# A written-out program order for every engine in the attention part of a fused attention and mixture-of-experts kernel

## The chip, the cores and the metric

The kernel runs on one core of a Trainium2 chip. The metric is the device time of one execution in microseconds (us), the median over several executions.

The engines are named as in the profile: PE is TensorE (PEld its weight loads), DVE is VectorE, ACT is ScalarE, POOL is GpSimd, and SP is the queue that issues most DMA transfers. Each engine takes its instructions in one order; engines wait for each other through semaphores.

## The reference

A decaying linear attention over 4 batches, 8 heads, 768 positions and head size 48, in float32, feeds a mixture of 8 experts of which each token takes one.

```python
def _attn_ref(q, k, v, alpha):
    for t in range(S):
        state = alpha[:, :, t, :, None] * state + np.einsum('bhd,bhe->bhde', k[:, :, t], v[:, :, t])
        y[:, :, t] = np.einsum('bhd,bhde->bhe', q[:, :, t], state)
...
def _moe_ref(x, modality_id, w_gate, modality_bias, w1, w2):   # x: 3072 tokens of 384
    logits = x @ w_gate + modality_bias[modality_id]
    e_idx = np.argmax(logits, axis=1)
    ...
    for e in range(E):                                         # 8 experts, 384 -> 1024 -> 384
        mask = e_idx == e
        h = np.maximum(x[mask] @ w1[e], 0.0)
        out[mask] = gate_w[mask, None] * (h @ w2[e])
```

## The kernel before

**The attention part** works in 12 steps (PS). A step s takes 128 positions of two batches, all 16 heads of them; six steps (NC) make one sequence, so the state starts afresh at steps 0 and 6. The 16 heads lie as eight tiles (KS) of two heads, in two halves of four tiles (NP). For each step the kernel does the following, and the loop of lines 811 to 851 runs the stages of different steps side by side:

- `decay(s)` on DVE: a backward scan of the decays into G (L238, its second operand is the table DR in SBUF), the reciprocals of the segment totals into DF (L239), a forward scan into Fw (L240), and the two products kh = k times G and qh = q times Fw (L241, L242).
- `scores(s-1)`: PE multiplies qh and kh (L259), ACT copies the four PSUM banks to scT (L262), and POOL zeroes the upper triangle of each half (L263).
- `keys(s-1)`: PE transposes kh (L272), ACT copies it to knat (L273).
- `from_state(s-1)` and `states(s-1)`: PE multiplies qh with the decayed state UB (L301), then forms the update kv from knat and v (L322). DVE adds it to the state, S (L332, or L334 at the start of a sequence), and `decayed(s)` multiplies S by the segment's decay into UB (L286).
- `from_values(s-1)`: PE multiplies scT with v (L345) into two banks named y.
- for step s-2: `outputs` (ACT copies y to yt, L357), `rows` (PE transposes yt, L368; ACT copies it to xs, L369; SP stores it to the scratch xd, L371), `logits_turned` (L376, copied as lts, L378) and `logits` (PE L384, and DVE adds the parts up in L, L385).
- `guard(s)` on ACT: an activation over all of alpha, tile X (L246, result junk), and a copy of the segment totals (L249, amin). They feed a check for decays out of range (`out_of_range`, L701 to L708) that decides on a slow path.

X has three buffers; kt and qt have two, vt three. `load` issues their refills on SP.

**Routing** runs inside the same loop for groups of 128-token tiles: `route_group` (six small DVE instructions), `route_ranks` (PE and about nine DVE instructions), `route_early`, `early_places`, and the early gathers and weight loads for the first two expert slots. Steps 5, 8, 10 and 11 carry a group each; steps 10 to 12 carry the early slots.

**The expert part** then runs 12 full slots and a half one: split weights into two float32r parts on ACT and DVE, three matmuls for each product on PE, and a scatter of the output by POOL.

**What sets the order.** The program goes through a planner that orders each engine's instructions by its own estimate of when their inputs are there. Only PE is taken out of its hands, from step 2 on: `pin` marks an instruction to be kept in the order in which it is written. DVE, ACT, POOL and SP stand as the planner put them. PSUM has eight banks: four named tr (scores, transposes, first expert layer), two y, one kv and one rt (small results of the routing and the logits).

```python
    for s in range(PS + 1):
        mark["pin"] = s > 1
```

Of the kernel before, what the change touches and what calls it, by code (L numbers as in the profile page):

```python
# [21 lines left out]
P = 128  # L22
# [35 lines left out]

@with_exitstack
def attention_moe(ctx: ExitStack, tc: tile.TileContext, q, k, v, alpha, at_, kt_, qt_, vt_, mid, wg, wgp_, mb, w1, w2, out):  # L60
    nc = tc.nc
    vec, act, pool, pe, sp = nc.vector, nc.scalar, nc.gpsimd, nc.tensor, nc.sync
# [42 lines left out]

    def first_layer(j, z):
        if z == 0:
            hps.append(bank(2, T))
        f = 256 * j + P * z
        for d in range(ND):  # L110
            pin(pe.matmul(hps[j][:, z], WR[0][0][:, d, f : f + P], xf[:, d], start=(d == 0), stop=(d == ND - 1)))

    def first_inputs():
        for d0, d1 in ((0, 2), (2, 3)):
            xp = ps.tile([P, 2, T], F32, name="kv") if d0 == 0 else bank(1, T)
            for d in range(d0, d1):
                for u in range(2):
                    pin(pe.transpose(xp[:, d - d0, u * P : (u + 1) * P], xg[0][:, u, d * P : (d + 1) * P], ident))
            act.copy(xf[:, d0:d1], xp)

    def pin(ins):

        if mark.get("pin"):
            tc.keep_in_program_order(ins)
        return ins
# [33 lines left out]
    DR = ac.tile([P, KS * SEG + 1], F32, name="DR")  # L159
    vec.memset(DR, AFLOOR)  # L160
    vec.memset(DR[:, SEG :: SEG], 1.0)
# [64 lines left out]
    def parts(s):  # L226
        return (slice(0, NP), slice(NP, KS)) if s == 0 else (slice(0, KS),)

    def decay(s):
        x = X[s % NX_]  # L230
        G = sb.tile([P, KS * SEG + 1], F32, name="G")
        Fw = sb.tile([P, KS * SEG], F32, name="Fw", bufs=1)
        kh = sb.tile([P, KS, P], F32, name="kh")
        qh = sb.tile([P, KS, P], F32, name="qh")
        for z in parts(s):
            f = slice(z.start * SEG, z.stop * SEG)
            r = slice(z.start * SEG + 1, z.stop * SEG + 1)
            vec.tensor_tensor_scan(G[:, r][:, ::-1], x[:, r][:, ::-1], DR[:, r][:, ::-1], 0.0, op0=ALU.mult, op1=ALU.max)  # L238
            vec.reciprocal(DF[:, f][:, 0::SEG], G[:, r][:, 0::SEG])  # L239
            vec.tensor_tensor_scan(Fw[:, f], x[:, f], DF[:, f], 0.0, op0=ALU.mult, op1=ALU.add)  # L240
            vec.tensor_tensor(kh[:, z], KT[s % NB][:, z], seg(G[:, 1:], 1, z), op=ALU.mult)  # L241
            vec.tensor_tensor(qh[:, z], QT[s % NB][:, z], seg(Fw, 1, z), op=ALU.mult)  # L242
        st[s, "G"], st[s, "k"], st[s, "q"] = G, kh, qh

# [6 lines left out]
    def scores(s):  # L251
        kh, qh = st[s, "k"], st[s, "q"]
        st[s, "s"] = []
        for z in range(2):
            pp = [bank(NP, P) for _ in range(2)]
            for j in range(NP):
                for g in range(2):
                    r = slice(64 * g, 64 * g + D)
                    pin(pe.matmul(pp[g][:, j], kh[r, NP * z + j], qh[r, NP * z + j], start=True, stop=True))  # L259
# [6 lines left out]
    def keys(s):  # L266
        if s % NC < NC - 1:
            kn = sb.tile([P, 2, NP, P], F32, name="knat")
            for z in range(2):
                p = bank(NP, P)  # L270
                for j in range(NP):
                    pin(pe.transpose(p[:, j], st[s, "k"][:, NP * z + j], ident))  # L272
# [15 lines left out]
    def from_state(s):  # L288
# [3 lines left out]
        if s % NC > 0:  # L292
            qh, U = st[s, "q"], UB[s % 2]
            for z in range(2):
                for a in range(2):
                    for o in range(2):
                        for g in range(2):
                            x, j = g ^ o, 2 * a + o
                            k = NP * z + j
                            pin(  # L300
                                pe.matmul(  # L301
                                    yof(yk, z, x, j), U[halves[g], k], qh[halves[g], k], start=new(s, o, x), stop=False
                                )
                            )
# [7 lines left out]
    def states(s):  # L312
        if s % NC < NC - 1:
            kn, vt = st[s, "n"], VT[s % NV]
            kv = ps.tile([P, KS, D], F32, name="kv")
            for z in range(2):
                for j in range(NP):
                    for g in range(2):
                        h = DM * z + D * head(j, g)
                        r = halves[g]  # L320
                        pin(
                            pe.matmul(  # L322
                                kv[r, NP * z + j],
                                kn[:, z, j, r],
                                vt[:, h : h + D],
                                start=(z == 0 and j == 0),
                                stop=(z == 1 and j == NP - 1),
                            )
                        )
# [5 lines left out]
            st[s + 1, "S"] = S1  # L335

    def from_values(s):
        yk, vt = st[s, "yp"], VT[s % NV]
        for z in range(2):
            for j in range(NP):  # L340
                for x in range(2):
                    g = x ^ j % 2
                    h = DM * z + D * head(j, g)
                    pin(
# [4 lines left out]
                            start=new(s, j % 2, x),  # L349
                            stop=(z == 1 and j > 1),  # L350
                        )
                    )

    def outputs(s):
        yt = sb.tile([P, 2, NP, P], F32, name="yt")
        for z in range(2):
# [6 lines left out]
    def rows(s):  # L363
        xs = sb.tile([P, 2, DM], F32, name="xs")
        for z in range(2):
            p = bank(NP, P)
            for j in range(NP):
                pin(pe.transpose(p[:, j], st[s, "yt"][:, z, j], ident))  # L368
            act.copy(xs[:, z].rearrange("p (j x d) -> p j x d", j=NP, x=2), p.rearrange("p j (x e) -> p j x e", x=2)[:, :, :, :D])  # L369
        i = 2 * s  # L370
        sp.dma_start(xd[row(i) : row(i) + 2 * P].rearrange("(z t) d -> t z d", z=2), xs)  # L371

    def logits_turned(s):
        lt = ps.tile([P, 2, P], F32, name="rt")
        for j in range(NP):
            pin(pe.matmul(lt[32 * j : 32 * j + 32], wgp[:, j], st[s, "yt"][:, :, j], start=True, stop=True))  # L376
# [4 lines left out]
    def logits(s):  # L381
        lp = ps.tile([P, 2, P], F32, name="rt")
        for c in range(2):
            pin(pe.transpose(lp[:, c], st[s, "l"][:, c], ident))  # L384
# [4 lines left out]
    def logits_pe(i, xs, wgs):  # L389
# [5 lines left out]
        lp = ps.tile([P, E], F32, name="rt")  # L395
# [51 lines left out]
    def route_ranks(t0, t1):  # L447
# [10 lines left out]
        rp = ps.tile([P, n, E], F32, name="rt")  # L458
# [669 lines left out]
```

## Time and profile before

| | us |
|---|---|
| median of three runs | 415.29 |
| lowest and highest run | 414.42, 416.45 |
| the profiled execution, its own time | 416.15 |
| its span, first to last instruction | 414.40 |
| PE busy over the span | 350.1 |
| DVE busy | 271.7 |
| ACT busy | 205.2 |
| POOL busy | 130.8 |

The mean granted clock of PE is 0.942 of full speed. A busy time is the sum of an engine's instructions over the span; it averages over the attention part, where no engine is full, and the expert part, where PE is. So the parts have to be read apart.

### The profile page before, as it was taken

What the parts mean: (1) busy time and instruction counts of PE and PEld (TensorE: products, weight loads), DVE (VectorE), ACT (ScalarE), POOL (GpSimd) and SP (SyncE); (2) the same over time, 40 slices, a digit from 0 to 9 for tenths busy, and PEclk for the clock granted to TensorE, in tenths of its full rate; (3) what the DMA queues carried; (4) which work ended last, traced back from release to release, by engine and by line L of the source; (5) the groups of instructions that cost most, each with busy time, mean ns of one, the idle gap of its engine ahead of it and who ended that gap; (6) DMA issues with size and microseconds to landing.
All of it is one profiled execution on the core that took longest, in us unless ns stands there. A gap on an engine that the chain in (4) does not pass through costs nothing. (4 is left out here: it accounts for less than half of the span.)

```text
span 414.4 us, 8601 instructions
## 1 busy us (share of the span) xinstructions
PE 350.1 (84%) x3370; PEld 325.3 (79%) x3370; DVE 271.7 (66%) x444; ACT 205.2 (50%) x366; POOL 130.8 (32%) x137
## 2 busy tenths in 40 slices
PE   0648695777679599979989999999999999999980
PEld 0547584656558577759989999999999999999980
DVE  5999874977289965279598566484755848445120
ACT  2346553524355445436378456474664747535230
POOL 7124430212124304341866433323333231221000
PEclk9969986888689989999999999999999999999996
DMA  7987654466324129912999593855838467221000
GB/s 278 322 198 189 169 153 116 125 182 177 92 91 130 49 85 368 352 39 73 378 384 365 212 356 110 317 175 207 291 118 332 157 243 249 100 93 38 21 24 7
DMA packets 38933, 76.31 MB, mean 184 GB/s; under 512 B 4293, under 2 KB 20842, under 8 KB 38884
## 3 DMA queue, kind: packets, MB, share of 16 engines
q1 hardware_dynamic: 34788, 65.83, 49.1%
q0 software_dynamic: 4096, 9.85, 6.4%
q8 instruction: 28, 0.46, 0.4%
q14 instruction: 21, 0.17, 0.1%
HBM read 66.22 MB, written 9.65 MB: 183 GB/s over the span
## 5 line engine op out<-in xcount | busy, mean ns | idle before, releaser
L263 POOL TENSOR_SCALAR_AFFINE_SELECT scT<-scT 128x1024 f32<-128x1024 f32 x24 | 38.1, 1602 | 117.5 <-ACT scT L262 112.0
L934 PE MATMUL tr<-xL,w1H 128*128 128x256 f32 x264 | 73.7, 283 | 1.1 <-DVE xL L898 1.1
L935 PE MATMUL tr<-xH,w1L 128*128 128x256 f32 x264 | 73.4, 283 | 0.0
L933 PE MATMUL tr<-xH,w1H 128*128 128x256 f32 x264 | 72.4, 282 | 0.0
L907 DVE TENSOR_TENSOR w1L<-w1r,w1H 128x768 fp32r<-128x768 f32 x44 | 42.0, 966 | 46.3 <-ACT w1H L905 45.8
L957 PE MATMUL y<-w2H,hH 128*128 128x384 f32 x192 | 65.5, 341 | 0.0
L959 PE MATMUL y<-w2H,hL 128*128 128x384 f32 x192 | 64.4, 335 | 0.0
L958 PE MATMUL y<-w2L,hH 128*128 128x384 f32 x192 | 64.3, 335 | 0.0
L875 POOL DMA_INDIRECT out_dram<-os,odx x24 | 26.7, 1112 | 104.1 <-ACT os L962 99.1
L907 DVE TENSOR_TENSOR w2L<-w2r,w2H 128x768 fp32r<-128x768 f32 x52 | 49.3, 956 | 11.4 <-ACT w2H L905 9.8
L934 PEld LDWEIGHTS tr<-xL,w1H 128*128 128x128 f32 x264 | 50.3, 191 | 1.4 <-DVE xL L898 1.4
L935 PEld LDWEIGHTS tr<-xH,w1L 128*128 128x128 f32 x264 | 50.3, 191 | 0.0
L933 PEld LDWEIGHTS tr<-xH,w1H 128*128 128x128 f32 x264 | 50.0, 191 | 0.0
L905 ACT CAST w1H<-w1r 128x768 fp32r<-128x768 f32 x44 | 36.0, 835 | 26.6 <-PE tr L934 26.6
L905 ACT CAST w2H<-w2r 128x768 fp32r<-128x768 f32 x52 | 42.9, 836 | 12.2 <-PE y L959 12.2
L940 DVE SCALAR_TENSOR_TENSOR hL<-tr,hH 128x512 fp32r<-128x512 f32 x48 | 32.7, 683 | 14.1 <-ACT hH L937 14.0
L259 PE MATMUL tr<-qh,kh 48*128 48x128 f32 x384 | 27.0, 293 | 14.0 <-DVE qh L242 14.0
L937 ACT ACTIVATE hH<-tr 128x512 fp32r<-128x512 f32 x48 | 28.6, 595 | 18.0 <-PE tr L935 11.8
L259 PEld LDWEIGHTS tr<-qh,kh 48*128 48x128 f32 x384 | 24.3, 201 | 16.4 <-DVE qh L242 14.3
L683 POOL DMA_INDIRECT xg<-xd,idx x26 | 28.6, 1099 | 27.2 <-PE tr L895 22.0
L957 PEld LDWEIGHTS y<-w2H,hH 128*128 128x128 f32 x192 | 36.1, 188 | 0.5 <-issue 0.5
L958 PEld LDWEIGHTS y<-w2L,hH 128*128 128x128 f32 x192 | 36.1, 188 | 0.0
(209 smaller groups left out, 615.1 us busy)
## 6 DMA issues: line engine op xcount, KB each, us to landing
w1r<-in_w_dram SPq DMA_DIRECT2D x26, 768.0 KB, 6.4
w2r<-in_w_dram SPq DMA_DIRECT2D x26, 768.0 KB, 8.8
vt<-in_paired_v_dram SPq DMA_DIRECT2D x12, 384.0 KB, 4.2
xd<-xs SPq DMA_DIRECT2D x12, 384.0 KB, 3.1
X<-in_turned_alpha_dram SPq DMA_DIRECT2D x18, 193.7 KB, 3.5
kt<-in_turned_k_dram SPq DMA_DIRECT2D x18, 192.0 KB, 3.5
qt<-in_turned_q_dram SPq DMA_DIRECT2D x18, 192.0 KB, 4.1
X<-in_turned_alpha_dram SPq DMA_DIRECT2D x2, 516.5 KB
```

Source lines behind the costliest of these rows:

```text
L259: pin(pe.matmul(pp[g][:, j], kh[r, NP * z + j], qh[r, NP * z + j], start=True, stop=True))
L263: pool.affine_select(sc, sc, [[0, 2], [0, NP], [1, P]], ALU.is_ge, 0.0, base=0, channel_multiplier=-1)
L683: pool.indirect_dma_start(xg[i % NX][:, u], None, xd[0:rows], ix, bounds_check=rows - 1, oob_is_err=False)
L905: act.copy(hi, src)
L907: vec.tensor_tensor(lw, src, hi.bitcast(F32), op=ALU.subtract)
L933: pe.matmul(hp[:, z], wH[:, d, fs], xH[:, d], start=(d == 0), stop=False)
L934: pe.matmul(hp[:, z], wH[:, d, fs], xL[:, d], start=False, stop=False)
L935: pe.matmul(hp[:, z], wL[:, d, fs], xH[:, d], start=False, stop=(d == ND - 1))
L940: mark[f"h{j}L"] = vec.scalar_tensor_tensor(hL, hp, 0.0, hH.bitcast(F32), op0=ALU.max, op1=ALU.subtract)
L957: pe.matmul(op, hH[:, z, us], wH[:, z], start=(f == 0), stop=False)
L958: pe.matmul(op, hH[:, z, us], wL[:, z], start=False, stop=False)
L959: pe.matmul(op, hL[:, z, us], wH[:, z], start=False, stop=(f == NF - 1))
```

## The change

All five engines' handles are wrapped so that every instruction that the attention part and its routing write is kept in program order, until the last route count is written. The order itself is then laid out anew:

- within a step, DVE now does the state sum and UB first, then the backward scan in two halves, the totals, the forward scan, the logits' sum, and the scaled keys and queries in two halves; routing work has four fixed places in a step;
- PE does the logits' transposes ahead of `from_values`;
- the check `guard` runs for step s-1 instead of s, and stands at the end of the step, as do the store of xd and the refill of X;
- the check's summary `out_of_range` moves behind the last logits;
- the table DR of the backward scan becomes bfloat16, covers half a step, and lies in the PSUM bank that rt had; the small results take banks of tr as long as the order is kept;
- `from_values` finishes one bank of y before the other, and `outputs` copies bank by bank.

```diff
+class Ordered:
...
+        def call(*a, **kw):
+            ins = f(*a, **kw)
+            if self.on and hasattr(ins, "ins"):
+                self.tc.keep_in_program_order(ins)
+            return ins
...
-    vec, act, pool, pe, sp = nc.vector, nc.scalar, nc.gpsimd, nc.tensor, nc.sync
+    order = [1]
+    vec, act, pool, pe, sp = (Ordered(e, tc, order) for e in (nc.vector, nc.scalar, nc.gpsimd, nc.tensor, nc.sync))
...
+    def small(p, *shape):
+        if order:
+            return ps.tile([p, *shape], F32, name="tr", bufs=4)
+        return ps.tile([p, *shape], F32, name="rt")
...
-    DR = ac.tile([P, KS * SEG + 1], F32, name="DR")
-    vec.memset(DR, AFLOOR)
-    vec.memset(DR[:, SEG :: SEG], 1.0)
+    DR = ps.tile([P, NP * SEG], BF16, name="rt")
+    dr16 = ac.tile([P, NP * SEG], BF16, name="dr16")
+    vec.memset(dr16, AFLOOR)
+    vec.memset(dr16[:, P::SEG], 1.0)
+    vec.tensor_copy(DR.bitcast(F32), dr16.bitcast(F32))
...
-            vec.tensor_tensor_scan(G[:, r][:, ::-1], x[:, r][:, ::-1], DR[:, r][:, ::-1], 0.0, op0=ALU.mult, op1=ALU.max)
...
+    def back(s, z):
+        x, G = X[s % NX_], st[s, "G"]
+        r = slice(z.start * SEG + 1, z.stop * SEG + 1)
+        vec.tensor_tensor_scan(G[:, r][:, ::-1], x[:, r][:, ::-1], DR[:, ::-1], 0.0, op0=ALU.mult, op1=ALU.max)
+
+    def totals(s, z):
...
+        vec.reciprocal(DF[:, f][:, 0::SEG], st[s, "G"][:, r][:, 0::SEG])
+
+    def forth(s, z):
...
+    def scaled(s, z):
+        vec.tensor_tensor(st[s, "k"][:, z], KT[s % NB][:, z], seg(st[s, "G"][:, 1:], 1, z), op=ALU.mult)
+        vec.tensor_tensor(st[s, "q"][:, z], QT[s % NB][:, z], seg(st[s, "F"], 1, z), op=ALU.mult)
...
+    def state(s):
+        if s % NC > 0:
             S1 = sb.tile([P, KS, D], F32, name="S")
-            if s % NC > 0:
-                vec.tensor_tensor(S1, UB[s % 2][:, :, :D], kv, op=ALU.add)
+            kv = st[s - 1, "kv"]
+            if s % NC > 1:
+                vec.tensor_tensor(S1, UB[(s - 1) % 2][:, :, :D], kv, op=ALU.add)
             else:
                 vec.tensor_copy(S1, kv)
...
-        for z in range(2):
+        for o in range(2):
             act.copy(
-                yt[:, z].rearrange("p (a o) t -> p o a t", o=2),
-                st[s, "yp"][:, :, 2 * P * z : 2 * P * (z + 1)].rearrange("p o (a t) -> p o a t", a=2),
+                yt.rearrange("p z (a o) t -> p o z a t", o=2)[:, o],
+                st[s, "yp"][:, o].rearrange("p (z a t) -> p z a t", z=2, a=2),
             )
...
-        lt = ps.tile([P, 2, P], F32, name="rt")
+        lt = small(P, 2, P)
...
         if na:
             first_layer(3, 1)
-            mark["pin"] = False
+            order.clear()
...
     for s in range(PS + 1):
-        mark["pin"] = s > 1
-        if s + 2 < PS:
-            load(s + 2, "a")
         if 0 < s and s + 1 < PS:
             load(s + 1, "kqv")
         if 0 <= s - 2:
             outputs(s - 2)
-        run(s, 0)
-        if s < PS:
-            decay(s)
+        if s == 0:
+            begin(0)
+            for z in (Z0, Z1):
+                back(0, z)
+                totals(0, z)
+                forth(0, z)
+                scaled(0, z)
         if 0 <= s - 1:
             scores(s - 1)
+            state(s - 1)
+            decayed(s - 1)
+        if 0 < s < PS:
+            begin(s)
+            back(s, Z0)
+            back(s, Z1)
+            totals(s, ZZ)
+        run(s, 0)
+        if 0 < s < PS:
+            forth(s, ZZ)
+        if 0 <= s - 1:
             keys(s - 1)
-        run(s, 1)
         if s == PS:
             first_inputs()
         if 0 <= s - 2:
             rows(s - 2)
             logits_turned(s - 2)
+        run(s, 1)
         if 0 <= s - 1:
             from_state(s - 1)
             states(s - 1)
-        if s < PS:
-            decayed(s)
-        run(s, 2)
+        if 0 <= s - 2:
+            logits(s - 2)
+        if 0 < s < PS:
+            scaled(s, Z0)
+            scaled(s, Z1)
         if s == PS:
             first_layer(0, 0)
             first_layer(0, 1)
         if 0 <= s - 1:
             from_values(s - 1)
-        if s < PS:
-            guard(s)
+        run(s, 2)
+        if 0 <= s - 1:
+            guard(s - 1)
         if 0 <= s - 2:
-            logits(s - 2)
+            store(s - 2)
+        if s + 2 < PS:
+            load(s + 2, "a")
+        run(s, 3)
...
-    out_of_range()
     outputs(PS - 1)
...
     first_layer(2, 0)
+    logits(PS - 1)
+    store(PS - 1)
+    out_of_range()
     first_layer(2, 1)
-    logits(PS - 1)
```

## Rows read from the trace of the kernel before

**Rows 1.** Stretches: PE, PEld, DVE, ACT, POOL busy us (instructions); clock, DMA share, GB/s
```profile
60.00:70.00 10.00, 5.45 (x95) 4.58 (x95) 4.37 (x5) 3.04 (x7) 2.47 (x2) 0.78 0.47 115
...
31.00:173.00 142.00, 113.38 (x1659) 93.50 (x1658) 102.78 (x175) 66.03 (x144) 38.21 (x26) 0.88 0.55 160
...
190.00:402.50 212.50, 211.20 (x1523) 210.69 (x1522) 128.42 (x177) 118.48 (x184) 74.75 (x68) 1.00 0.58 207
```

**Rows 2.** Who waited for whom: total us, times, longest
```profile
ACT junk L246 <- DMA X<-in_turned_alpha_dram: 24.8, 9, 5.2
ACT amin L249 <- DVE G L238: 15.2, 6, 5.4
```

**Rows 3.** Timeline, 65 to 72 us: start, length, engine, line, last wait
```profile
65.49 1.16 ACT L246 ACTIVATE junk<-X,bhi 128x1033 bf16<-128x1033 uint32 x1 [5.20 <-DMA X<-in_turned_alpha_dram]
66.64 0.56 ACT L273 COPY knat<-tr 128x512 f32<-128x512 f32 x1
67.26 1.10 PE L322 MATMUL kv<-vt,knat 128*64 128x48 f32 x16 [4.55 <-ACT knat L273]
68.15 3.65 PE L345 MATMUL y<-scT,vt 128*64 128x128 f32 x32
68.40 0.55 DVE L332 TENSOR_TENSOR S<-UB,kv 128x384 f32<-128x384 f32 x1 [4.85 <-PE kv L322]
```

**Rows 4.** Timeline of PE, and of ACT's score copies, 127 to 137 us
```profile
127.43 2.06 PE L259 MATMUL tr<-qh,kh 48*128 48x128 f32 x32
...
129.14 2.04 ACT L262 COPY scT<-tr 128x512 f32<-128x512 f32 x4
...
129.78 1.14 PE L272 MATMUL tr<-ident,kh 128*128 128x128 f32 x8 [0.29 <-ACT scT L262]
...
134.40 1.93 PE L345 MATMUL y<-scT,vt 128*64 128x128 f32 x32
136.26 0.44 PE L384 MATMUL rt<-ident,lts 128*128 128x128 f32 x2
136.63 0.60 PE L259 MATMUL tr<-qh,kh 48*128 48x128 f32 x6
```

**Rows 5.** Groups of DVE instructions by shape: busy us, mean ns of one
```profile
L240 DVE TENSOR_TENSOR_SCAN Fw<-X,DF 128x1032 f32<-128x1032 f32 x11 | 26.3, 2387 | 0.2
L238 DVE TENSOR_TENSOR_SCAN G<-X,DR 128x1032 f32<-128x1032 f32 x11 | 25.4, 2305 | 0.6
...
L286 DVE TENSOR_TENSOR UB<-S,G 128x384 f32<-128x384 f32 x10 | 5.5, 555 | 0.2
...
L332 DVE TENSOR_TENSOR S<-UB,kv 128x384 f32<-128x384 f32 x8 | 4.4, 548 | 9.9 <-PE kv L322 9.9
```

**Rows 6.** Timeline of DVE and POOL, 34 to 39 us and 89 to 91 us
```profile
34.42 4.74 POOL L263 TENSOR_SCALAR_AFFINE_SELECT scT<-scT 128x1024 f32<-128x1024 f32 x2 [6.43 <-ACT scT L262]
...
36.16 2.05 DVE L241 TENSOR_TENSOR kh<-kt,G 128x1024 f32<-128x1024 f32 x1
...
89.56 1.21 DVE L241 TENSOR_TENSOR kh<-kt,G 128x1024 f32<-128x1024 f32 x1
...
90.75 1.10 POOL L263 TENSOR_SCALAR_AFFINE_SELECT scT<-scT 128x1024 f32<-128x1024 f32 x1 [13.67 <-ACT scT L262]
```

**Rows 7.** Timeline of DVE, route_ranks of six tiles: first and last of seven
```profile
121.16 0.20 DVE L468 TENSOR_TENSOR rk<-rt,oh 128x48 f32<-128x48 f32 x1
...
121.92 0.95 DVE L480 TENSOR_TENSOR OL<-ioh,lo 128x768 f16<-128x768 f16 x1
```

**Rows 8.** Timeline: the first scans, scores of steps 1 and 11, the last logits
```profile
6.46 2.36 DVE L238 TENSOR_TENSOR_SCAN G<-X,DR 128x516 f32<-128x516 f32 x2 [2.08 <-DMA X<-in_turned_alpha_dram]
...
31.07 2.26 PE L259 MATMUL tr<-qh,kh 48*128 48x128 f32 x32
...
162.49 2.06 PE L259 MATMUL tr<-qh,kh 48*128 48x128 f32 x32
...
173.02 0.44 PE L384 MATMUL rt<-ident,lts 128*128 128x128 f32 x2
```

More of the change, by code (lines that the diff above doesn't have):

```diff
@@ L56, with __init__, __getattr__ @@
 GROUPS = ((0, 6), (6, 12), (12, 16), (16, 18), (18, 22), (22, 24))
+class Ordered:
+    def __init__(self, engine, tc, on):
+        self.engine, self.tc, self.on = engine, tc, on
+    def __getattr__(self, name):
+        f = getattr(self.engine, name)
+        def call(*a, **kw):
[3 more added lines that the diff above has]
+            return ins
+        return call if callable(f) else f
 @with_exitstack
@@ L224, in seg, with begin @@
         return t.rearrange("p (a b) -> p a b", b=SEG)[:, z, lo : lo + P]
[L226 to L237, printed above, removed]
-            vec.tensor_tensor_scan(G[:, r][:, ::-1], x[:, r][:, ::-1], DR[:, r][:, ::-1], 0.0, op0=ALU.mult, op1=ALU.max)
[L239 to L243, printed above, removed]
+    Z0, Z1, ZZ = slice(0, NP), slice(NP, KS), slice(0, KS)
+    def back(s, z):
[3 more added lines that the diff above has]
+    def totals(s, z):
+        r = slice(z.start * SEG + 1, z.stop * SEG + 1)
+        f = slice(z.start * SEG, z.stop * SEG)
+        vec.reciprocal(DF[:, f][:, 0::SEG], st[s, "G"][:, r][:, 0::SEG])
+    def forth(s, z):
+        f = slice(z.start * SEG, z.stop * SEG)
+        vec.tensor_tensor_scan(st[s, "F"][:, f], X[s % NX_][:, f], DF[:, f], 0.0, op0=ALU.mult, op1=ALU.add)
+    def scaled(s, z):
+        vec.tensor_tensor(st[s, "k"][:, z], KT[s % NB][:, z], seg(st[s, "G"][:, 1:], 1, z), op=ALU.mult)
+        vec.tensor_tensor(st[s, "q"][:, z], QT[s % NB][:, z], seg(st[s, "F"], 1, z), op=ALU.mult)
+    def begin(s):
+        st[s, "G"] = sb.tile([P, KS * SEG + 1], F32, name="G")
+        st[s, "F"] = sb.tile([P, KS * SEG], F32, name="Fw", bufs=1)
+        st[s, "k"] = sb.tile([P, KS, P], F32, name="kh")
+        st[s, "q"] = sb.tile([P, KS, P], F32, name="qh")
     def guard(s):
@@ L299, in from_state @@
                             k = NP * z + j
[L300 to L304, printed above, removed]
+                            pe.matmul(yof(yk, z, x, j), U[halves[g], k], qh[halves[g], k], start=new(s, o, x), stop=False)
     def new(s, o, g):
@@ L348, in from_values @@
                             st[s, "s"][z][:, g, j],
-                            start=new(s, j % 2, x),
+                            start=new(s, o, x),
                             stop=(z == 1 and j > 1),
                         )
-                    )
     def outputs(s):
         yt = sb.tile([P, 2, NP, P], F32, name="yt")
-        for z in range(2):
+        for o in range(2):
             act.copy(
-                yt[:, z].rearrange("p (a o) t -> p o a t", o=2),
-                st[s, "yp"][:, :, 2 * P * z : 2 * P * (z + 1)].rearrange("p o (a t) -> p o a t", a=2),
+                yt.rearrange("p z (a o) t -> p o z a t", o=2)[:, o],
+                st[s, "yp"][:, o].rearrange("p (z a t) -> p z a t", z=2, a=2),
             )
@@ L394, in logits_pe @@
         act.copy(xc, xt)
-        lp = ps.tile([P, E], F32, name="rt")
+        lp = small(P, E)
         for c in range(ND):
@@ L539, in route_early @@
         n = EARLY[s]
-        cnt = ps.tile([P, E], F32, name="rt")
-        pin(pe.matmul(cnt, ones, ohs, start=True, stop=(s == 0)))
+        cnt = small(P, E)
+        pe.matmul(cnt, ones, ohs, start=True, stop=(s == 0))
         if s:
-            pin(pe.matmul(cnt, ones, left, start=False, stop=True))
+            pe.matmul(cnt, ones, left, start=False, stop=True)
         vec.tensor_reduce(base, cnt, axis=AX.X, op=ALU.max)
@@ L572, in early_places @@
         n = EARLY[s]
-        tp = ps.tile([P, 2], F32, name="rt")
+        tp = small(P, 2)
         for t in range(n):
-            pin(pe.matmul(tp, OL[:, t], OHE[:, t], start=(t == 0), stop=(t == n - 1)))
+            pe.matmul(tp, OL[:, t], OHE[:, t], start=(t == 0), stop=(t == n - 1))
         places(tp, slice(2 * s, 2 * s + 2))
@@ L621, in route_end @@
         vec.tensor_copy(meta[:, na:NS], kp[0:1, 1, 0:nh:2])
[L622 removed]
+        tp = small(P, nh)
         for g in range(3):
@@ L788, in run @@
             f(*a)
-    def early(e):
-        early_places(e)
-        gather(e, row(EARLY[e]))
     def early_gates():
```

89 lines of the change are left out of this document (42 added, 47 removed).

## The prediction

> **What bounds the kernel now.** I read the busy time by stretches first [rows 1]. From 190 us to the end PE is busy 211.2 of 212.5 us at full clock: the expert part is PE's, and the change does not touch its instructions. What can move is the time until then. Between 31 and 173 us no engine is full: PE 113.4 of 142 us, at a granted clock of 0.88, DVE 102.8, ACT 66.0. So the attention is a ring of waits, and the question is which.
>
> The list of waits names it [rows 2]. ACT waited nine times, 24.8 us in all, for a load of X before the check `guard`, and 15.2 us for a scan before the check's second copy. Nothing in the attention needs the check. But ACT is one queue, and the key copies stand behind it. The timeline shows one case whole [rows 3]: ACT sat 5.20 us until X had landed, did the check, then knat; PE's kv matmuls had waited 4.55 us for knat, and DVE 4.85 us for kv. A check that nobody needs yet stopped three engines. Its second cost is the clock: the value matmuls behind that stall took 3.65 us, against 1.93 us where PE had not stalled [rows 3, 4], and the stretch has a granted clock of 0.78 [rows 1], a mix of PE's two levels, 1.2 and 2.4 GHz.
>
> **What the change does to these waits.** `guard(s-1)` reads an X that the scans of the step before have already used, and stands behind all of its step's copies. Its 1.2 us of ACT stay, but it waits for no load and nothing urgent stands behind it. The refill of X goes behind it on SP, so it starts later within a step, but has a whole further step before its backward scan. `out_of_range`, whose first DVE instruction needs every step's check, goes to the tail. In return every engine now runs in lock step, so I lay out one plain step (no routing) engine by engine.
>
> *PE.* The eight groups of one step, undisturbed, run from 127.43 to 136.63 us, of which 0.29 is a wait [rows 4]: 8.9 us. All but the value matmuls and the logits' transposes are done 6.7 us after the scores begin (134.40 less 127.43 less 0.29); the transposes, now next, take 0.4 (136.26 to 136.63): 7.1 us.
>
> *DVE.* S 0.55, UB 0.56, backward scan 2.31 (two halves of about 1.2 each, by the pair in [rows 8]), totals about 0.2, forward scan 2.31 (its mean of 2.39 holds one disturbed instruction), the logits' sum about 0.2, scaled keys and queries 2 by 1.21 [rows 6] and an estimate of 0.05 more for each half, 2.6 [scans and sums from rows 5, the small ones at the length of those in rows 7]: 8.7 to 8.8 us.
>
> *The loop between them.* The logits' sum now stands ahead of the scaled products in DVE's queue, so a late PE holds back DVE: 7.1 us + sum 0.2 + keys and queries of the first half 1.3 = 8.6 us until the next scores may start. All three loops come to 8.6 to 8.9 us; with 0.3 for the hops, an estimate, a plain step takes 9.2.
>
> *ACT* had 66.0 us in these eleven steps, 6 us each [rows 1], and *POOL* less; SP moves the same bytes in less time: 160 GB/s over 142 us becomes about 190 over 120, and the expert part does 207 over 212 us [rows 1]. All three are covered; if ACT's cover were gone, its round would have to grow by 3 us to show.
>
> **The table in PSUM.** POOL's triangles and DVE collide now [rows 6]: two triangles took 4.74 us together, and the keys' product beside them 2.05 us, against 1.21 undisturbed. That is 0.85 us for a triangle, twice in a step if DVE then runs products or the forward scan. In my layout ACT has the scores' halves ready 2.1 and 3.2 us into the step, (half the scores 1.0, then two copies of about 0.53 for each half [rows 4]), and a triangle alone takes 1.1 [rows 6]: they end at 4.3. The backward scan, after 0.75 us of products and 1.1 of S and UB that reach into the step, runs from 1.9 to 4.3; so both triangles fall beside it. No row shows a scan that reads PSUM. Bounds from rows: below, no collision and no longer scan (the sum S, which reads PSUM, takes 548 ns, UB, of the same shape and from SBUF alone, 555 [rows 5]); above, both collisions stay, 1.7 us a step. I take the lower, as S is the nearest row.
> The Trainium skill (SBUF — State Buffer, "SBUF: two separate sides") says that a VectorE instruction with two SBUF inputs and a GpSimd one exclude each other for their whole length; with one input in PSUM the scan would be free of it, as in the lower bound. By that rule the sum stays as below; [rows 6] agree with the exclusion itself. The skill's VectorE: DVE Perf Modes (the errata section) also gives a PSUM source 62 cycles more than an SBUF one; on the two halves that is an estimate of 0.13 us a step, 1.4 us in all, which the S and UB rows do not show.
>
> **The sum.** Scores of step 1 start at 31.07 us now, since ACT's queue stood behind the check there too. After: DVE starts at 6.46 [rows 8], needs 2 by 3.95 us (scan 1.2, total 0.2, scan 1.2, products 1.3) for step 0 and 6.3 for the first half of step 1: 20.6 us. PE, cold there, starts the second scores at 14.4 and has half the scores, keys, kv and values ahead: 4.8 us at full clock, 9.1 at the ratio 3.65 to 1.93, so 23.5. I take 23.
>
> From there: six plain steps (2, 3, 4, 6, 7, 9) at 9.2 = 55.2. Step 3 also does the bias table and half index, nine small instructions, an estimate of 2.2. Steps 5, 8 and 10 carry a group on DVE, which has no slack: `route_group` six at about 0.2 = 1.2, `route_ranks` 121.16 to 122.87 = 1.7 [rows 7] and one sum 0.2, so 3.1 each: 3 by 12.3 = 36.9. Step 11 has the previous step's `route_early` behind it (about twelve at 0.2 = 2.4), a small group (2.7) and `early_places` (1.4): 15.7. Step 12 has no scans and is PE's: it took 162.49 to 173.02 = 10.5 [rows 8] and keeps its work. Together 23 + 55.2 + 2.2 + 36.9 + 15.7 + 10.5 = 143.5 us for the end that stands at 173.0 now: 29.5 us less.
>
> A check on that: DVE's busy time between 31 and 173 us is 102.8 [rows 1]. After the change it also has one step's scans and products (about 8.6) behind the new start of 23, less some 5 of collisions: 23 + 106 = 129 if it never waited, and then PE's last step, mostly alone, 9: 138 us. My layout leaves 5 us of waits over the floor.
>
> The tail keeps its work: three more first-layer blocks, the last rows, the counts. The small results now compete with the first layer's four held banks for tr. A wait there is at most for one ACT copy or one DVE pass at a time; I put it at nothing, covered by first-layer matmuls that need no new bank, and at 3 us at worst.
>
> Profiled time 416.15 (span 414.40; 0.9 above the median of 415.29) less 29.5 gives 386.6; I say 386.
>
> **Rivals.**
> *Collisions stay.* The triangles come later than laid out, beside the forward scan or the products, or the scan from PSUM is no freer: 1.7 us on DVE's round. Six plain steps go from 9.2 to about 10.6 (8.4), five others lose 1.7 (at most 7): 386 + 15 = 401. For it: ACT must copy the outputs ahead of the scores, and any delay shifts the triangles. Against: a triangle that already runs when the forward scan comes holds it only for its rest.
> *The waits move.* X or k, q, v come late, now that SP's queue is in order too, and a blocked refill holds back the next. If DVE got back all 24.8 us that ACT waits now: 386 + 25 = 411. Against: a refill has over a step, while the longest wait of now is 5.2 us.
> *PE falls to the lower level and stays.* In lock step PE may idle a little in every step; at 1.2 GHz a round costs 8.9 by 1.89 = 16.8 us, 7.6 more than planned. Four plain steps so give back the 29.5 us, so from there it is no faster, and all six give 386 + 46 = 432: slower. For it: granted 0.78 at 60 to 70 us. Against: that came with idle stretches of 4.5 us, and the layout has PE idle 0.3 us in a plain step; the expert part keeps 1.00.
> *No change:* the planner already had this order; the 24.8 us of waits exclude it.
>
> **Chances and range.** Layout holds 0.65 (its own range 379 to 394: floor 138 at the near side, 0.7 us more a step at the far), collisions 0.18, moved waits 0.10, lower clock 0.05, anything else 0.02. The range 378 to 405 takes in the first two and leaves out about 0.17. A measurement tells 0.5%, 2.1 us, from no change. Faster 0.92, the same 0.03, slower 0.05, the slower from the clock.
>
> **What would show it.** No wait of ACT for X; scores of neighbouring plain steps about 9.2 us apart and about 12.3 at steps 5, 8, 10; scores of step 1 near 23 us; last logits' transposes or values of step 12 near 143 us; backward halves near 1.2 us with POOL's triangles at 1.1 us beside them; granted clock near 1.0 from 30 us on. Wrong if DVE's list of waits shows loads or PE above 10 us in all, or if a product's halves still take 1 us each instead of 0.65.

## The result, and the profile after

The changed kernel takes 385.45 us, the median of three runs (384.64 to 388.58), against 415.29 before: a ratio of 0.930, 95% interval 0.921 to 0.939. Beside five further runs on another chip it was 0.935 (0.932 to 0.938). The profiled execution is the median one; its span is 383.3 us. A few executions take over 1.5% longer than the fastest of their kernel: the ratios leave them out, and of the traces below only that of the logits behind the values is of such a one.

In this profile every instruction stands at L67, the line of the wrapper, so it is read by tiles. The stretches come first (columns as in [rows 1]):

```profile
0.00:31.00 31.00, 18.32 (x256) 16.19 (x258) 25.16 (x34) 12.19 (x24) 12.57 (x40) 1.00 0.82 267
31.00:40.17 9.17, 9.17 (x161) 7.73 (x156) 8.70 (x12) 6.37 (x14) 2.14 (x2) 1.00 0.86 216
31.00:143.00 112.00, 98.38 (x1533) 82.70 (x1528) 98.84 (x213) 64.87 (x143) 28.36 (x25) 0.97 0.75 211
22.44:139.47 117.03, 103.41 (x1662) 87.13 (x1661) 106.84 (x223) 68.59 (x150) 30.13 (x26) 0.97 0.77 213
160.00:372.00 212.00, 210.37 (x1518) 209.65 (x1516) 127.07 (x174) 118.86 (x185) 72.97 (x68) 1.00 0.59 207
```

The expert part (last row) is what it was: 210.4 of 212 us on PE, as in [rows 1]. The attention is another thing. DVE did 102.8 us of work in 142 before, and now does 98.8 in 112; the granted clock rose from 0.88 to 0.97. The fourth row runs from the scores of step 1 to the end of step 12, and holds the same matmuls as the 142 us of [rows 1] (1662 records and 1659). PE is busy for 103.4 us in it instead of 113.4 and idle for 13.6 instead of 28.6: of the 25 us by which these steps are shorter, 15 were waits and 10 are shorter matmuls, in line with the higher clock. In a plain step, 31 to 40 us, PE is busy for all of its 9.17 us and DVE for 8.70: the ring of waits has turned into two nearly full engines, PE a little the fuller.

The starts of the scores give the time of each step. The timeline of PE shows the scores of steps 1, 2, 3, 4, 5, 10 and 11, and then the value matmuls of step 12, the end of the attention:

```profile
22.44 2.06 PE L67 MATMUL tr<-qh,kh 48*128 48x128 f32 x32
...
31.26 2.15 PE L67 MATMUL tr<-qh,kh 48*128 48x128 f32 x32
...
40.17 2.15 PE L67 MATMUL tr<-qh,kh 48*128 48x128 f32 x32
...
51.48 2.36 PE L67 MATMUL tr<-qh,kh 48*128 48x128 f32 x32 [1.81 <-DVE qh L67]
...
62.99 2.27 PE L67 MATMUL tr<-qh,kh 48*128 48x128 f32 x32 [0.76 <-DVE qh L67]
...
111.19 2.60 PE L67 MATMUL tr<-qh,kh 48*128 48x128 f32 x32 [0.37 <-DVE qh L67]
...
127.59 2.06 PE L67 MATMUL tr<-qh,kh 48*128 48x128 f32 x32
...
137.50 1.97 PE L67 MATMUL y<-scT,vt 128*64 128x128 f32 x32
```

Read pairwise: 8.8 and 8.9 us for plain steps, 11.3 for the step with the bias table, 11.5 for a routed step, 16.4 for step 11, and the end at 139.5 us (137.50 + 1.97), where the values of step 12 ended at 173 before, as the last logits start [rows 8]. In the list of waits, ACT's wait for X [rows 2] is gone, and DVE's waits for PE in this stretch come to 4.2 us; its first scan's wait for X at the start, 3.8 us once, is its only one for a load. With the products' halves at 0.69 us, neither of the two signs by which the prediction would have been wrong came in the attention. The rows for 31 to 143 us:

```profile
PE tr L67 <- DVE oh L67: 7.0, 4, 3.3
...
PE tr L67 <- DVE qh L67: 5.0, 5, 1.8
...
DVE L L67 <- PE tr L67: 2.1, 5, 0.5
```

### The profile page after: what moved, and what is told of

The parts are those of the page before. It is cut to its first block, busy times and chain, and to the rows that moved or that the text cites. A ratio compares the mean times of both kernels' runs of the same rounds, so it can differ in the third digit from the quotient of the medians.

```text
span 383.3 us, 8638 instructions
## 1 busy us (share of the span) xinstructions
PE 339.7 (89%) x3370; PEld 318.6 (83%) x3370; DVE 264.6 (69%) x478; ACT 204.5 (53%) x366; POOL 119.0 (31%) x137
## 5 line engine op out<-in xcount | busy, mean ns | idle before, releaser
L67 PE MATMUL tr<-xL,w1H 128*128 128x256 f32 x264 | 73.9, 283 | 1.2 <-DVE xL L67 1.2
L67 DVE TENSOR_TENSOR w1L<-w1r,w1H 128x768 fp32r<-128x768 f32 x44 | 42.0, 965 | 46.3 <-ACT w1H L67 45.7
L67 PE MATMUL tr<-xH,w1L 128*128 128x256 f32 x264 | 73.6, 283 | 0.0
L67 PE MATMUL tr<-xH,w1H 128*128 128x256 f32 x264 | 72.7, 283 | 0.0
L67 PE MATMUL y<-w2H,hH 128*128 128x384 f32 x200 | 68.5, 343 | 0.0
L67 PE MATMUL y<-w2L,hH 128*128 128x384 f32 x200 | 67.3, 337 | 0.0
L67 PE MATMUL y<-w2H,hL 128*128 128x384 f32 x200 | 67.2, 336 | 0.0
L67 POOL DMA_INDIRECT out_dram<-os,odx x24 | 25.2, 1052 | 107.8 <-ACT os L67 86.5
L67 DVE TENSOR_TENSOR w2L<-w2r,w2H 128x768 fp32r<-128x768 f32 x52 | 49.6, 957 | 11.3 <-ACT w2H L67 9.8
L67 POOL TENSOR_SCALAR_AFFINE_SELECT scT<-scT 128x1024 f32<-128x1024 f32 x24 | 29.7, 1247 | 85.9 <-ACT scT L67 85.1
L67 PEld LDWEIGHTS tr<-xL,w1H 128*128 128x128 f32 x264 | 50.4, 191 | 1.4 <-DVE xL L67 1.4
L67 DVE SCALAR_TENSOR_TENSOR hL<-tr,hH 128x512 fp32r<-128x512 f32 x50 | 34.1, 684 | 24.3 <-ACT hH L67 24.2
L67 PEld LDWEIGHTS tr<-xH,w1L 128*128 128x128 f32 x264 | 50.3, 191 | 0.0
L67 ACT CAST w1H<-w1r 128x768 fp32r<-128x768 f32 x44 | 36.0, 834 | 26.6 <-PE tr L67 26.6
L67 PEld LDWEIGHTS tr<-xH,w1H 128*128 128x128 f32 x264 | 50.1, 191 | 0.0
L67 ACT CAST w2H<-w2r 128x768 fp32r<-128x768 f32 x52 | 42.9, 834 | 10.7 <-PE y L67 10.7
L67 PE MATMUL tr<-qh,kh 48*128 48x128 f32 x384 | 28.7, 295 | 17.8 <-DVE qh L67 17.6
L67 PEld LDWEIGHTS tr<-qh,kh 48*128 48x128 f32 x384 | 25.3, 199 | 20.7 <-DVE qh L67 13.0
L67 ACT ACTIVATE hH<-tr 128x512 fp32r<-128x512 f32 x50 | 29.8, 596 | 21.6 <-PE tr L67 19.2
L67 POOL DMA_INDIRECT xg<-xd,idx x26 | 28.3, 1089 | 34.7 <-PE tr L67 22.3
L67 PEld LDWEIGHTS y<-w2H,hH 128*128 128x128 f32 x200 | 37.9, 190 | 0.5 <-issue 0.5
L67 PEld LDWEIGHTS y<-w2L,hH 128*128 128x128 f32 x200 | 37.9, 190 | 0.0
```

The costliest lines, as they stand in the source:

```text
L67: ins = f(*a, **kw)
```

## The experiments

Twelve kernels ran in three groups, each group on one chip beside the kernel before. The chips differ (before: 419.56, 414.75 and 419.82 us), so all comparisons below are of ratios to the kernel before on the same chip. Ratios can differ by some 0.005 from chip to chip: the changed kernel itself has 0.930 on one and 0.935 on another. The first two groups ask which part of the change carries the gain; the third asks about its tail.

**Order alone.** The kernel before with its statements as they stand and all five engines kept in that order; the table stays in SBUF, the small results stay in rt.

```diff
-    vec, act, pool, pe, sp = nc.vector, nc.scalar, nc.gpsimd, nc.tensor, nc.sync
+    order = [1]
+    vec, act, pool, pe, sp = (Ordered(e, tc, order) for e in (nc.vector, nc.scalar, nc.gpsimd, nc.tensor, nc.sync))
```

> The kernel before, its statements where they stood, but all five engines kept in program order; the check of step s still stands at the end of step s, the table stays in SBUF, the small results keep their own bank. Theory A (what cost the time was ACT waiting for loads of X inside the check, and any order in which the check comes behind its step's work removes that): ACT waits for X under 4 us in all instead of 24.8, plain steps of 9.2 to 10.5 us, 388 to 402 us. Rival B (the new layout of the statements and the table in PSUM carry the gain): 405 us or more, with DVE or PE waits of several us in each step.

Measured 0.998 (0.995 to 1.001): no gain. Yet ACT no longer waits for X inside the attention, and plain steps take 8.9 to 9.6 us, a little more than in the changed kernel. All of it is lost in the routed steps, 17.5 to 21 us each. Its list of waits has a row that came to 0.3 us before:

```profile
PE rt L67 <- DVE rk L67: 18.9, 4, 7.0
```

The timeline of step 5 shows how it comes about:

```profile
60.15 0.24 PE L67 MATMUL rt<-oh,tri 128*128 128x48 bf16 x1
...
62.45 2.04 DVE L67 TENSOR_TENSOR kh<-kt,G 128x1024 f32<-128x1024 f32 x1
64.41 1.21 DVE L67 TENSOR_TENSOR qh<-qt,Fw 128x1024 f32<-128x1024 f32 x1
65.55 0.19 DVE L67 TENSOR_TENSOR rk<-rt,oh 128x48 f32<-128x48 f32 x1
...
65.80 1.08 PE L67 MATMUL rt<-yt,wgp 128*32 128x256 f32 x8 [3.97 <-DVE rk L67]
```

PE fills the one rt bank with ranks at 60.15. In the kept order DVE reads them only behind the forward scan and both products, at 65.55. Until then PE cannot start the next tenant of the bank, the turned logits, and everything written behind them stands still. The granted clock falls to 0.64 in that step, 54.67 to 73.15 us, which lengthens it further.

**Order, and the small results in the tr banks.** Order alone, with every small result taking a bank of tr instead of rt.

```diff
+    def small(p, *shape):
+        if order:
+            return ps.tile([p, *shape], F32, name="tr", bufs=4)
+        return ps.tile([p, *shape], F32, name="rt")
...
-        rp = ps.tile([P, n, E], F32, name="rt")
+        rp = small(P, n, E)
```

> The run with the old statements and all engines in order, with one thing more: the small results take banks of tr instead of the one bank rt. In that run plain steps took 8.9 to 9.6 us, but the steps with routing 17.5 to 21, and there PE waited four times, up to 7.0 us, for DVE to read the ranks out of rt, which stood behind both scans and products. Theory A (that one bank is what cost the routed steps): routed steps 12 to 14 us, 396 to 405 us, no such wait. Rival B (the order of DVE's statements costs it, whatever bank): 412 us or more, PE then waits elsewhere for DVE.

Measured 0.960 (0.957 to 0.964). The wait for the bank is gone; from the scores of step 4 to those of step 6, a routed step and the plain one behind it, 22.3 us pass instead of 27.3. With the order kept, these few lines are worth 0.038, some 16 us (the two ratios are from different chips).

**The table in SBUF.** The changed kernel, with the halved bfloat16 table left in SBUF.

```diff
-    DR = ps.tile([P, NP * SEG], BF16, name="rt")
-    vec.tensor_copy(DR.bitcast(F32), dr16.bitcast(F32))
+    DR = dr16
```

> The changed kernel with the table of the backward scan (same bfloat16 half table) in SBUF. Theory A (the two triangles then collide with the backward scan, 0.85 us each): 9 to 18 us more than the changed kernel, 394 to 403 us, triangles of 1.5 to 2.5 us instead of 1.1. Rival B (the triangle only waits, and the scores have time to spare): within 2 us of the changed kernel, 383 to 388 us.

Measured 0.953 (0.947 to 0.960), that is 0.018 to 0.024 more than the changed kernel, 8 to 10 us. The groups of DVE and POOL instructions by shape, 31 to 143 us (busy us, mean ns of one), first of the changed kernel:

```profile
L67 DVE TENSOR_TENSOR_SCAN G<-X,rt 128x516 f32<-128x516 f32 x18 | 21.1, 1211 | 0.0
L67 DVE TENSOR_TENSOR_SCAN Fw<-X,DF 128x1032 f32<-128x1032 f32 x9 | 20.8, 2306 | 0.2
...
L67 POOL TENSOR_SCALAR_AFFINE_SELECT scT<-scT 128x1024 f32<-128x1024 f32 x20 | 23.7, 1193 | 73.0 <-ACT scT L67 72.3 <-ACT knat L67 0.5
```

and then of the one with the table in SBUF:

```profile
L67 DVE TENSOR_TENSOR_SCAN G<-X,dr 128x516 f32<-128x516 f32 x18 | 27.1, 1548 | 0.0
L67 DVE TENSOR_TENSOR_SCAN Fw<-X,DF 128x1032 f32<-128x1032 f32 x9 | 22.6, 2512 | 0.2
...
L67 POOL TENSOR_SCALAR_AFFINE_SELECT scT<-scT 128x1024 f32<-128x1024 f32 x20 | 32.9, 1657 | 73.0 <-ACT scT L67 72.8
```

A half of the backward scan is 0.34 us longer there, the forward scan 0.21 and a triangle 0.46, with the same work. For a step's DVE that is 2 by 0.34 + 0.21 = 0.9 us, and eleven steps make about 10. The steps agree: from the scores of step 1 to those of step 11 pass 115.9 us in this trace and 105.2 in that of the changed kernel. Step 12 is 3.9 us longer too, by a chance of timing that the changed kernel also meets (see the tail), so it is not put down to the table. The Trainium skill (SBUF — State Buffer, "SBUF: two separate sides") says that a VectorE instruction with two SBUF inputs and a GpSimd instruction lock each other out; both sides grow here, as it says, and with the scan's table in PSUM they do not (1.21 us a half, 1.19 a triangle).

**The check's place alone.** The kernel before with `guard(s-1)` and the refill of X at the end of the step and the summary late; the planner still orders ACT.

```diff
-        if s + 2 < PS:
-            load(s + 2, "a")
...
-        if s < PS:
-            guard(s)
+        if 0 <= s - 1:
+            guard(s - 1)
+        if s + 2 < PS:
+            load(s + 2, "a")
```

> The kernel before with only the check moved: check of step s-1 instead of s, the refill of X behind it, the check's summary behind the last logits; the planner still orders DVE, ACT, POOL and SP. Theory A: the 24.8 us of ACT waits for X go and most of the gain comes without any order, 390 to 402 us. Rival B (the planner's order costs by itself, and puts other waits in their place): 405 us or more, with a new wait of ACT or DVE of over 10 us in the list.

Measured 0.998 (0.995 to 1.001): nothing. Its list of waits:

```profile
ACT junk L246 <- DMA X<-in_turned_alpha_dram: 23.0, 8, 4.2
```

and its timeline:

```profile
50.85 1.16 ACT L246 ACTIVATE junk<-X,bhi 128x1033 bf16<-128x1033 uint32 x1 [4.17 <-DMA X<-in_turned_alpha_dram]
...
55.00 2.31 DVE L238 TENSOR_TENSOR_SCAN G<-X,DR 128x1032 f32<-128x1032 f32 x1
...
57.62 0.22 ACT L249 COPY amin<-G 128x8 f32<-128x8 f32 x1
```

The check is written a step later than the scan whose input it reads, and ACT runs it 4 us ahead of that scan, as soon as X has landed. So the edit did not do what it was for: a place in the text is not a place in the queue when a planner orders the queue, and this run says nothing of a check that really runs late.

**The whole layout, with PE's order alone.** All statements, tiles and banks of the changed kernel, but only PE kept in order.

```diff
-    vec, act, pool, pe, sp = (Ordered(e, tc, order) for e in (nc.vector, nc.scalar, nc.gpsimd, nc.tensor, nc.sync))
+    vec, act, pool, sp = nc.vector, nc.scalar, nc.gpsimd, nc.sync
+    pe = Ordered(nc.tensor, tc, order)
```

> The changed kernel, its statements and the table in PSUM as they are, but only PE kept in program order; the planner orders DVE, ACT, POOL and SP. Theory A (the place of the check is what counts, and the planner finds about the same order from these statements): 385 to 395 us. Rival B (the order kept on the other engines is what counts): 400 us or more, with ACT or DVE waits of over 10 us in all that the changed kernel does not have.

Measured 1.0115 (1.008 to 1.015): 1% longer than before, with the table in PSUM and all. Its list of waits has ACT's wait for X back, as long as in [rows 2], and PE waits for the score copies behind it:

```profile
ACT junk L272 <- DMA X<-in_turned_alpha_dram: 25.4, 8, 4.7
...
PE tr L67 <- ACT scT L288: 19.5, 8, 5.8
```

**No check.** The kernel before without `guard`; planner as before.

```diff
-        if s < PS:
-            guard(s)
+    pool.memset(gacc, 0.0)
+    pool.memset(amin, 1.0)
```

> The kernel before without the check over alpha: the activation and the copy of the totals in every step are left out, and the two tiles that they fill are set to harmless constants once. The planner orders DVE, ACT, POOL and SP as before. Theory A (the check ahead in ACT's queue is what costs the time; the moved check gained nothing only because the planner pulled it forward again, as its ACT waits of 23.0 us for X show): 388 to 400 us. Rival B (without the check other waits of the planner's order end last in its place): 408 us or more, and new waits of ACT or DVE over 10 us in all.

Measured 0.953 (0.948 to 0.957), 18.4 us by the medians (414.75 to 396.36). That is what the check costs before in all: its waits in ACT's queue, its own 1.2 us a step, and the buffers of X that it holds. The run does not part these.

**ACT's order alone.** The kernel before, with only ACT kept in program order.

```diff
+    act = Ordered(nc.scalar, tc, order)
```

> The kernel before, statements and places as they were, with ACT kept in program order beside PE; DVE, POOL and SP stay with the planner. Theory A (it is ACT's queue alone): ACT waits under 4 us for X, 390 to 402 us. Rival B (DVE's and SP's order by the planner cost as much): 408 us or more.

Measured 0.972 (0.968 to 0.976), 10 us, with the check in place and one engine's order fixed; ACT's wait for X inside the steps is gone. The 404.44 us lie between the two theories' ranges: ACT's order gives back over half of what the check costs, and the rest stays open.

**The logits behind the values.** The changed kernel with the logits' transposes behind `from_values`, and so the products behind the logits' sum later too.

```diff
-        if 0 <= s - 2:
-            logits(s - 2)
-        if 0 < s < PS:
-            scaled(s, Z0)
-            scaled(s, Z1)
...
             from_values(s - 1)
+        if 0 <= s - 2:
+            logits(s - 2)
+        if 0 < s < PS:
+            scaled(s, Z0)
+            scaled(s, Z1)
```

> The changed kernel with the logits' transposes behind the value matmuls on PE again, and DVE's scaled products still behind the logits' sum. Theory A (the loop PE, logits' sum, scaled products, next scores is as long as the step): every plain step 1.5 to 1.9 us longer, 10.4 to 10.8 instead of 8.9 us, in all 10 to 17 us over the changed kernel, a ratio to the kernel before of 0.955 to 0.97. Rival B (DVE has slack there): ratio 0.925 to 0.935.

Measured 0.970 (0.966 to 0.975): 0.035 to 0.040 more than the changed kernel, 15 to 17 us. Its list of waits, 31 to 160 us, shows where; the size is taken from the ratio alone:

```profile
PE tr L67 <- DVE qh L67: 16.3, 10, 1.9
```

PE now waits for qh ahead of ten steps' scores, where the changed kernel has 5 such waits and 5.0 us. So the loop PE to logits' sum to products to the next scores is real: lengthened by the value matmuls, it sets the step. Part of the cost comes through the clock behind these waits: the granted clock is 0.939 to 0.955 in the executions that the ratio goes by, and 0.973 to 0.977 in those of the changed kernel on the first chip.

**The tail.** From the end of the last value matmuls to the first of the unbroken expert matmuls, before takes 17.2 us (173.0 to 190.3) and after 19.5 (139.5 to 159.0): 2.3 us are given back. The first of the unbroken matmuls, before and after:

```profile
190.26 0.44 PE L957 MATMUL y<-w2H,hH 128*128 128x384 f32 x1
```

```profile
158.99 0.44 PE L67 MATMUL y<-w2H,hH 128*128 128x384 f32 x1
```

Two theories: the small results compete for the tr banks; or the check's summary, now late in DVE's queue, holds up what stands behind it. One kernel put the tail's small results back into rt, one brought the summary ahead, one did both; the changed kernel ran again beside them. In the diff, the first two edits are those for rt (a third, not shown, keeps the logits in tr), the rest bring the summary ahead.

```diff
+        if order and len(order) == 1:
             return ps.tile([p, *shape], F32, name="tr", bufs=4)
...
+    order.append(1)
     outputs(PS - 1)
...
         if s == PS:
+            guard(s - 1)
...
+        if s == PS:
+            out_of_range()
         run(s, 2)
-        if 0 <= s - 1:
+        if 0 < s < PS:
             guard(s - 1)
...
-    out_of_range()
```

> The changed kernel again, unaltered, beside its variants on one chip: 382 to 389 us, a ratio to the kernel before of 0.92 to 0.94.

> The changed kernel, but behind the last step the ranks, the counts and the check's result take the bank rt again, which the table has left; the logits keep tr. From the last value matmuls to the unbroken expert matmuls the changed kernel takes 19.6 us (139.4 to 159.0), the kernel before 17.2 (173.0 to 190.2). Theory A (four banks for the first layer and the small results are too few): 1.5 to 2.5 us less than the changed kernel. Rival B (the summary of the check and what it holds back is the loss): within 0.7 us of it.

> The changed kernel, but the last step's check runs ahead of its value matmuls and the check's summary right behind them, instead of behind the last logits. Theory B (the summary holds back the tail: ACT's first relu of the expert part waited 2.37 us for it, PE 1.0 us, and the weight splits then fell between the last routing instructions on DVE): 1.5 to 3.5 us less than the changed kernel. Theory A (banks): within 0.7 us of it.

> Both edits of the tail together. If either theory holds alone, this equals the better of the two; if each has a part, it is 2 to 4 us under the changed kernel, a ratio to the kernel before of about 0.922 to 0.926 where the changed kernel has 0.93.

Measured: 0.935 (0.932 to 0.938) for the changed kernel, 0.925 (0.922 to 0.929) for rt, 0.925 (0.921 to 0.928) for the summary sooner, 0.923 (0.920 to 0.926) for both. The times alone would credit both theories. The traces do not: the tail took 19.7 us in the changed kernel, 20.1 with rt, 16.1 with the summary sooner and 16.6 with both. So the summary is worth some 3.5 us of tail, and the bank is worth nothing there. The changed kernel's tail (timeline):

```profile
146.51 0.24 DVE L67 TENSOR_REDUCE fl<-amin 128x1 f32<-128x96 f32 x1
...
146.78 0.60 ACT L67 ACTIVATE hH<-tr 128x512 fp32r<-128x512 f32 x1 [2.37 <-DVE fl L67]
...
147.26 0.18 PE L67 MATMUL tr<-flb,ones 128*128 128x1 bf16 x1 [1.01 <-DVE flb L67]
...
152.38 0.17 PE L67 MATMUL tr<-oh,tri 128*128 128x16 bf16 x1 [2.24 <-DVE oh L67]
```

and with the summary sooner:

```profile
139.20 0.18 PE L67 MATMUL tr<-flb,ones 128*128 128x1 bf16 x1
139.31 0.60 ACT L67 ACTIVATE hH<-tr 128x512 fp32r<-128x512 f32 x1 [4.57 <-PE y L67]
...
150.46 0.17 PE L67 MATMUL tr<-oh,tri 128*128 128x16 bf16 x1
```

ACT's first expert activation, hH, waited for the summary's fl and now starts 7.5 us sooner; PE's waits for flb and oh are gone. Part of the gain is the clock. The stretches of the two tails, the changed kernel's first:

```profile
139.47:158.99 19.52, 15.19 (x86) 12.05 (x86) 12.53 (x57) 10.03 (x21) 4.47 (x4) 0.91 0.16 57
```

```profile
139.27:155.34 16.07, 13.75 (x85) 10.82 (x86) 13.53 (x61) 8.89 (x18) 4.32 (x4) 1.00 0.21 73
```

From the counts that waited for oh to the unbroken matmuls pass 6.6 us (152.38 to 158.99) at a fallen clock, and 4.9 (150.46 to 155.34) with the summary sooner. Why hH has to wait for fl at all was not tried; that the expert tiles take the memory of the attention's tiles, the check's among them, would explain it, but is not shown.

What made the run with rt shorter than the changed kernel beside it lies elsewhere, in step 12. The timelines there, first of the changed kernel run again, then of the one with rt:

```profile
129.85 2.14 POOL L67 TENSOR_SCALAR_AFFINE_SELECT scT<-scT 128x1024 f32<-128x1024 f32 x2 [4.93 <-ACT scT L67]
129.88 1.08 DVE L67 TENSOR_SCALAR left<-taken 128x8 bf16<-128x8 f32 x1
130.88 1.14 DVE L67 SCALAR_TENSOR_TENSOR K<-taken,K 128x8 f32<-128x8 f32 x2
...
132.53 1.04 PE L67 MATMUL kv<-ident,xg 128*128 128x128 f32 x4 [3.20 <-DVE S L67]
```

```profile
129.54 0.17 DVE L67 TENSOR_SCALAR left<-taken 128x8 bf16<-128x8 f32 x1
129.62 0.23 DVE L67 SCALAR_TENSOR_TENSOR K<-taken,K 128x8 f32<-128x8 f32 x2
...
130.37 0.65 PE L67 MATMUL kv<-ident,xg 128*128 128x128 f32 x4 [1.07 <-DVE S L67]
```

Three bookkeeping passes of 8 columns came just behind the start of POOL's triangles in the first, and ahead of it (129.99 us) in the second. They took 2.2 us instead of 0.4; S, behind them, held back PE, and step 12 took 15.8 us instead of 11.9. The first profile of the same kernel, on the other chip, had the short form, as have the traces of the summary sooner and of both edits; the run with the table in SBUF had the long one. How often each form comes in the timed runs is not known, so the 0.010 between the changed kernel and the one with rt stays unsettled: this chance of timing explains it in the profiled runs, no more. The version with both edits beats the changed kernel, intervals apart (387.67 against 392.5 us on one chip); whether it beats the summary alone cannot be told.

## Why the prediction was right, point by point

It said 386.0 us, 378 to 405, and the time is 385.45. Its sum, term by term:

| | predicted us | measured us | difference |
|---|---|---|---|
| scores of step 1 start | 23 | 22.4 | -0.6 |
| six plain steps, bias table among them | 57.4 | 54.9 | -2.5 |
| routed steps 5, 8, 10 | 36.9 | 33.9 | -3.0 |
| step 11 | 15.7 | 16.4 | +0.7 |
| step 12 | 10.5 | 11.9 | +1.4 |
| end of the attention | 143.5 | 139.5 | -4.0 |
| tail against before | 0 | +2.3 | +2.3 |

The total is closer than its parts. That 4.0 us gained in the attention and 2.3 lost in the tail nearly cancel is luck; that every step lies within 1.4 us of its term is not.

- *The plain step.* 9.2 was taken, 8.3 to 9.1 measured: the estimate of 0.3 us for hops was not needed where an engine is full. The loops named are there. PE's own round binds in steps 2, 3, 7 and 9 (in step 3 it is busy for 8.91 of 8.91 us), DVE's in step 6, where PE has fewer matmuls (8.32 of 8.42), and the loop through the logits' sum binds as soon as it is lengthened (the logits behind the values).
- *Routed steps.* 3.1 us of DVE work were added on a DVE with no slack; 2.1 to 2.7 came on top, measured from 8.8. The term was oversized, its mechanism right: DVE is busy for 11.20 of the 11.51 us of step 5.
- *Step 12* was taken to be PE's alone. PE waits 1.07 us in it for S, which the kept order puts behind the bookkeeping of `early_places`: most of the 1.4.
- *Collisions.* The lower bound nearly held, and S was the right row to go by: a half takes 1.21 us and a triangle 1.19. What is left falls on UB, a mean of 0.70 us against 0.56 [rows 5], which still reads SBUF twice. The rival's price, 15 us, was too high: with the table in SBUF it is 8 to 10, 0.9 us a step and not 1.4 to 1.7. In that trace eight of ten pairs of backward halves lose about one triangle's length (3.20 us instead of 2.34), and the forward scan at most the rest of one (2.77 instead of 2.31 in step 3).
- *The tail* was put at nothing, with 3 us at worst, and the worst nearly came: +2.3. The fear named was a wait for a tr bank. The runs show the summary instead: `out_of_range` was costed as work without a waiter, and ACT's first hH waits for its fl.
- *The clock rival* came twice, in step 11 and in the tail, and not for good. In step 11 PE waited 3.27 us for oh, and the next groups ran long. The stretch and the timeline:

```profile
118.00:127.50 9.50, 7.47 (x103) 6.53 (x103) 8.50 (x28) 0.01 (x1) 2.31 (x2) 0.64 0.91 328
```

```profile
120.03 0.19 PE L67 MATMUL tr<-oh,tri 128*128 128x16 bf16 x1 [3.27 <-DVE oh L67]
...
120.20 1.99 PE L67 MATMUL y<-qh,UB 64*64 64x128 f32 x32
122.12 1.95 PE L67 MATMUL kv<-vt,knat 128*64 128x48 f32 x32
...
124.61 2.91 PE L67 MATMUL y<-scT,vt 128*64 128x128 f32 x32
```

The granted clock is 0.64, a mix of the two levels, and the values take 2.91 us against 1.97. In the next stretch it is 1.00 again.

The rest of the sum, 0.5 us, lies in the expert part and outside the span.

- *The opening theory* is right that the check costs, 18.4 us, and falls as a sufficient cause of the gain. The check's new place alone gives nothing, since the planner undoes it; the new layout under the planner takes 1% longer than before; and the fixed order alone gives nothing either, since it trades ACT's wait for X for PE's wait for the rt bank. The prediction did not see that wait as a rival: it costed the move of the small results to the tr banks only in the tail, as a possible loss. In the attention that move was worth 0.038, beside 0.047 for leaving out the check.

As ratios, the gain is built so: order alone 0.998; with the small results in tr 0.960; the whole change but for the table in PSUM 0.953; the whole change 0.930 to 0.935. So the halved products, the bank-by-bank outputs, the check's place and the new order within a step are together worth some 0.007, about what ratios across chips can tell, and the table 0.018 to 0.024. The parts do not add up: the order of all engines alone, the check's place alone, and the layout with only PE's order kept are each worth nothing or less.

## What to carry to other kernels

Where a planner orders a queue, moving a statement may change nothing until that order is kept (0.998 here); look at the trace for where the instruction really ran before crediting its new place. When an order is fixed by hand, look through every single-buffered tile that another engine frees: its reader's new place in that engine's queue can become the wait (18.9 us here). And a side task off the critical path has to be costed by who stands behind it, at the end of the program as in its loop.

## What the hardware showed beyond that

- A scan whose table lies in PSUM is as fast as one that reads SBUF alone: an undisturbed pair of halves took 2.34 us with the table in PSUM and 2.35 with the same bfloat16 table in SBUF (timelines of the changed kernel and of the one with the table in SBUF, below). The 0.13 us a step that the prediction worked out from the Trainium skill (VectorE: DVE Perf Modes, the errata section) do not appear.

```profile
33.07 2.34 DVE L67 TENSOR_TENSOR_SCAN G<-X,rt 128x516 f32<-128x516 f32 x2
```

```profile
47.72 2.35 DVE L67 TENSOR_TENSOR_SCAN G<-X,dr 128x516 f32<-128x516 f32 x2
```

- A collision between DVE and POOL does not scale with the size of the pass. A pass of 8 columns, 0.17 us alone, took 1.08 us beside a triangle (timelines of step 12 above). It ended at 130.96 us, about when the first of the two triangles did (129.85 and half of 2.14), so it paid the rest of the other's instruction, several times its own length.
- The granted clock does not tell all in the first step: 16 of the scores' matmuls took 2.08 us from 10.94 us on, where 32 took 2.06 from 22.44 us on, and the clock of 10.9 to 13.1 us reads 1.00.
